# A fused attention and two-layer mixture-of-experts kernel: the order of the gate chain in the first expert layer, its logits, its masks, and how one weight split is cut

## The chip, the cores and the metric

The kernel runs on one core of one Trainium2 chip. The metric is the device time of one execution in microseconds (us). Engines are called as the profile calls them: PE (TensorE, its weight loads apart as PEld), DVE (VectorE), ACT (ScalarE), POOL (GpSimd), SP (the queue that issues most DMAs).

## The reference

Three stages follow each other on 9984 tokens of 256 numbers.

```
scores = (1/S) * z @ z.T                      # S = 2496 tokens, 4 batches
x  = u * (relu(scores)**2 @ v)                # attention
skip = x @ w_skip > 0                         # layer 1: only tokens with skip
logits = x[skip] @ w_gate;  e = argmax;  p = softmax(logits)[e]
x[skip] += p * (relu(x @ w1[e]) @ w2[e])      # F = 1024 hidden, 8 experts
logits2 = x @ w_gate2 + bias[modality]        # layer 2: all tokens
e = argmax;  p = softmax(logits2)[e]
out = p * (relu(x @ w1b[e]) @ w2b[e])
```

The result of layer 1, y, is needed twice: it is added to the token's row, and its product with w_gate2 is added to the logits that the token brought along, which decide the token's expert in layer 2.

## The kernel before, in words

**Stages.** Attention comes first and sorts its tokens by expert into a list in memory, rows1 (tokens that skip layer 1 go to rows2 at once). Layer 1 then takes tiles of 348 rows of one expert (3 groups of 116), layer 2 takes tiles of 512 rows from rows2. All large products are made of three fp32r products of a high and a low half of each operand.

**A tile of layer 1** (`Moe.turn`, `Moe.work`). Two stages of eight parts each: ("h", f) computes block f of the hidden layer (`hidden`, six matmuls at line 766, then `hh` on ACT at 768 and `hl` on DVE at 769), ("o", f) adds block f to y (`out_part`, six matmuls at line 867). PE runs these in the order in which they are written. Between parts stand hooks, named in the dictionary `PLAN`: "next" loads the next tile's rows and w1, "w2" and "w1" split a quarter of the weights into halves (high on ACT, line 665; low of w2 on POOL and low of w1 on DVE, line 666), "x" transposes the next tile's rows (PE at 751, ACT at 755, DVE at 756), "load w2" loads the next w2, and "after" runs one further step of the generator `Moe1.after`.

**`Moe1.after`** finishes the tile before while the present one is computed. In order: copies of y out of PSUM as yS and yh (ACT, 877 and 878, the first instructions of a tile on ACT), the low halves yl (DVE, 881), the transposed logits lt (PE 885, ACT copy 887 to mlt), the rows of y (PE transposes at 894, DVE at 898 writes them into `x_out`; first two groups, then the third), the logits (PE transposes mlt at 904, ACT copy 906, DVE 908 to 910), the first maximum and the exponential (`FirstMax`, lines 109 to 118), the masks and sums of the expert's one-hot rows (920, `counted`, 129 to 136), then the row numbers (PE 148 to 158, DVE 174 to 181, 706). PE products of these steps take turns in two PSUM buffers named m.

**Sending.** `m1.send` stands at the top of the loop body and issues on POOL three scatters of the groups of `x_out` to rows2 (line 680, with small instructions at line 702 in front). The next tile's line 898 writes `x_out` again.

**The loop.** Layer 1 has 16 tiles: two written out in front of a hardware loop, 13 in the loop, one behind it. The last `after` runs inside the first tile of layer 2. Each engine follows its own list of instructions and waits on semaphores; at the end of the loop all engines meet.

**What the change touches.** `constants` (a new constant), `Shared.split` (line 666), `Moe1.PLAN`, `Moe1.after`, the dictionary of the tile in front of the loop, and the call of `m1.after` inside the first tile of layer 2.

Of the kernel before, what the change touches and what calls it, by code (L numbers as in the profile page):

```python
# [53 lines left out]
def constants(nc, pool):  # L54
    k = Consts()
    k.ones = pool.tile([128, 128], BF16, name="ones")
    nc.vector.memset(k.ones, 1.0)
    k.ident = pool.tile([128, 128], F32, name="ident")
    make_identity(nc, k.ident)
    diff = pool.tile([128, 128], F32, name="diff")  # L60
    nc.gpsimd.iota(diff, pattern=[[1, 128]], base=0, channel_multiplier=-1, allow_small_or_imprecise_dtypes=True)
    k.tri = pool.tile([128, 128], BF16, name="tri")
    nc.vector.tensor_scalar(k.tri, diff, 0.0, None, op0=ALU.is_gt)
    k.desc = pool.tile([128, E], F32, name="desc")
    nc.gpsimd.iota(k.desc, pattern=[[-1, E]], base=E, channel_multiplier=0, allow_small_or_imprecise_dtypes=True)
# [555 lines left out]
class Shared:  # L621
# [201 lines left out]
class Moe1(Moe):  # L823
# [5 lines left out]
        ("h", 3): [("w2", 1)],  # L829
        ("h", 4): [("w2", 2), ("after",), ("after",)],  # L830
# [38 lines left out]
    def after(self, lim, current, ps=None):  # L869
# [6 lines left out]
        for d in range(2):  # L876
            nc.scalar.copy(y[:, d], self.y[d])
            nc.scalar.copy(yh[:, d], self.y[d])
        for d in range(2):
            yield  # L880
            nc.vector.tensor_tensor(yl[:, d], y[:, d], yh[:, d].bitcast(F32), op=ALU.subtract)
        yield
        lt_ps = sh.ps_m.tile([2 * E, T], F32, name="m")
        for i, (d, m) in enumerate(((0, yh), (1, yh), (0, yl), (1, yl))):
            nc.tensor.matmul(lt_ps, self.wg[:, d], m[:, d], start=(i == 0), stop=(i == 3))
        lt = self.lt
        nc.scalar.copy(lt[:2 * E], lt_ps)
        yield
        x, xo = self.x_cur, self.x_out[:P]
        for g0 in range(0, G, 2):  # L890
            y_ps = sh.ps_m.tile([128, 2, D], F32, name="m")[:P]
            for g in range(g0, min(g0 + 2, G)):
# [4 lines left out]
            for g in range(g0, min(g0 + 2, G)):  # L897
# [4 lines left out]
        lg_ps = sh.ps_m.tile([128, G, 128], F32, name="m")[:P]  # L902
        for g in range(G):
            nc.tensor.transpose(lg_ps[:, g], lt[:, g * P:(g + 1) * P], k.ident)
        lo = s.tile([128, G, 2 * E], F32, name="mlo")[:P]
        nc.scalar.copy(lo, lg_ps[:, :, 0:2 * E])
        lg = s.tile([128, G, E], F32, name="mlg")[:P]
        nc.vector.tensor_tensor(lg, lo[:, :, 0:E], lo[:, :, E:], op=ALU.add)
        nc.vector.tensor_tensor(lg, lg, x[:, :, C_G1:C_G1 + 1].to_broadcast([P, G, E]), op=ALU.mult)
        nc.vector.tensor_tensor(lg, lg, x[:, :, C_B2:C_B2 + E], op=ALU.add)  # L910
        yield
        fm = FirstMax(nc, s, k, lg, P, G, "b")
        fm.exp()
        oh, sm = fm.hot, fm.total()
        nc.vector.tensor_copy(xo[:, :, C_TID], x[:, :, C_TID])
        nc.vector.reciprocal(xo[:, :, C_G2], sm)
        yield
        if current is not None:
            self.load_rows(current(), self.x_cur)
        nc.vector.tensor_copy(sh.lim, lim.rearrange("p t o -> p (t o)"))  # L920
        mk = self.counted(sh.lim)
        ohb, cum = first_max_done(nc, s, k, oh, mk, P, 1, G, "b")
        yield
        rks = row_counts(nc, s, ps or sh.ps_m, k, ohb, cum, P, 1, G, "b")
        at, mk = row_index(nc, s, rks, ohb, mk, self.carry, P, 1, G, "b")
        self.sc.index(at[:, 0], mk[:, 0])
# [102 lines left out]
def forward_kernel(ctx, tc, zT, v, uT, wg, wg2, mod, bias, w, out, nb=B, mode="reg_based"):  # L1029
# [36 lines left out]
    with ExitStack() as main:  # L1066
# [79 lines left out]
    m2.turn(lambda: (m2, e2, rb), m1.after(m1.table.lim[:, :, ds(n + 2, 1)], None, sh.ps_x), {  # L1146
# [83 lines left out]
```

## Time and profile before

| | |
|---|---|
| median of 3 runs | 1566.53 us (1563.34 to 1571.99) |
| the profiled execution | 1573.25 us |
| its span, first to last instruction | 1571.4 us |
| mean granted TensorE clock over the span | 0.981 |
| PE busy | 1494.9 us, 95% |
| DVE, ACT, POOL busy | 1070.2, 953.5, 598.7 us |
| loop of layer 1 | 795.66 to 1069.98 us of the span, 13 tiles |

All views of the profile come from the profiled execution, which is 6.7 us above the median. Times in the views are counted from the first instruction. A tile of layer 1 is counted here from its first copy of y on ACT (line 877).

### The profile page before, as it was taken

Reading aid. Unit: us, or ns where it says so; the run is one execution under the profiler, and the core shown is the slowest. Engines: PE = TensorE matmul, PEld = TensorE weight load, DVE = VectorE, ACT = ScalarE, POOL = GpSimd, SP = SyncE. Lnnn points to the kernel's source line nnn. Section 1 sums busy time; section 2 is a strip of 40 time slices with the busy share of each in tenths; the row PEclk is TensorE's granted clock in tenths of the full one; section 3 lists DMA queues with packets and bytes.
Section 4 is the critical chain, followed back from the end, with each engine's and each line's share of the span. In section 5 each row is a group of like instructions: output and inputs, shape, how many; then the busy total and the mean of one; then the engine's idle time right before and its main releaser. Section 6 shows DMA issues by size and latency. Waiting matters only on the chain. (4 is left out here: it accounts for less than half of the span.)

```text
span 1571.4 us, 34847 instructions
## 1 busy us (share of the span) xinstructions
PE 1494.9 (95%) x10972; PEld 1286.6 (82%) x10972; DVE 1070.2 (68%) x2562; ACT 953.5 (61%) x1729; POOL 598.7 (38%) x730
## 2 busy tenths in 40 slices
PE   7999999999999999998789898988999999999997
PEld 6878888888887887887788888888888888888886
DVE  7788887888788887776656666666755555545453
ACT  8777777777777777674455455554455455445452
POOL 2022333332222222333634445553553453454353
PEclk9999999999999999999899999999999999999999
DMA  9011211112111200031255444553443343443430
GB/s 356 28 41 56 68 39 44 51 50 91 33 42 61 69 28 27 31 93 49 85 173 158 141 149 151 158 156 107 157 153 128 131 146 124 135 143 121 151 130 23
DMA packets 49696, 160.24 MB, mean 102 GB/s; under 512 B 13285, under 2 KB 15195, under 8 KB 40384
## 3 DMA queue, kind: packets, MB, share of 16 engines
q1 hardware_dynamic: 28720, 124.24, 24.5%
q0 software_dynamic: 20736, 34.71, 6.4%
q8 instruction: 60, 0.98, 0.3%
q14 instruction: 36, 0.29, 0.1%
q10 hardware_dynamic: 144, 0.02, 0.0%
HBM read 124.24 MB, written 46.55 MB: 109 GB/s over the span
## 5 line engine op out<-in xcount | busy, mean ns | idle before, releaser
L680 POOL DMA_INDIRECT rows<-r,ix x160 | 205.3, 1283 | 347.5 <-DVE xs L341 276.1
L328 PE MATMUL o<-ah,vh 64*128 64x512 f32 (+1 forms) x1560 | 312.4, 386 | 9.2 <-DVE xs L341 9.2
L328 PE MATMUL o<-al,vh 64*128 64x512 f32 (+1 forms) x1560 | 304.5, 384 | 0.0
L328 PE MATMUL o<-ah,vl 64*128 64x512 f32 (+1 forms) x1560 | 302.9, 384 | 0.0
L769 DVE SCALAR_TENSOR_TENSOR hl<-ph,hh 128x512 fp32r<-128x512 f32 (+1 forms) x288 | 176.6, 614 | 164.1 <-ACT hh L768 163.1
L285 ACT ACTIVATE t<-s 128x1024 f32<-128x1024 f32 (+2 forms) x201 | 201.2, 1001 | 88.4 <-PE s L282 85.0
L299 DVE TENSOR_TENSOR al<-t,ah 128x1024 fp32r<-128x1024 f32 (+2 forms) x201 | 241.8, 1203 | 17.9
L666 POOL TENSOR_TENSOR w<-w2raw,w 128x512 fp32r<-128x512 f32 x144 | 183.7, 1292 | 179.8 <-issue 163.4
L768 ACT ACTIVATE hh<-ph 128x512 fp32r<-128x512 f32 (+1 forms) x288 | 155.8, 541 | 138.2 <-PE ph L766 118.9
L766 PE MATMUL ph<-mxh,zA 128*128 128x512 f32 (+1 forms) x576 | 217.8, 378 | 3.8 <-PEq L1226 1.8
L766 PE MATMUL ph<-mxh,zB 128*128 128x512 f32 (+1 forms) x576 | 212.4, 369 | 2.8 <-issue 2.8
L766 PE MATMUL ph<-mxl,zA 128*128 128x512 f32 (+1 forms) x576 | 212.6, 369 | 0.0
L297 ACT ACTIVATE t<-t 128x1024 f32<-128x1024 f32 (+2 forms) x201 | 208.1, 1036 | 5.7
L298 DVE CAST ah<-t 128x1024 fp32r<-128x1024 f32 (+2 forms) x201 | 137.1, 682 | 105.6 <-ACT t L297 103.5
L328 PEld LDWEIGHTS o<-ah,vh 64*128 64x128 f32 x1560 | 151.7, 185 | 44.4 <-DVE xs L341 16.8
L328 PEld LDWEIGHTS o<-al,vh 64*128 64x128 f32 x1560 | 151.4, 185 | 26.5
L328 PEld LDWEIGHTS o<-ah,vl 64*128 64x128 f32 x1560 | 148.0, 185 | 27.2
L867 PE MATMUL o<-hh,w 128*128 128x348 f32 x512 | 134.4, 346 | 8.3 <-POOL w L666 8.3
L766 PEld LDWEIGHTS ph<-mxh,zA 128*128 128x128 f32 x576 | 110.9, 193 | 23.6 <-issue 6.4
L282 PE MATMUL s<-zA,zB 64*128 64x512 f32 (+1 forms) x400 | 124.2, 389 | 0.0
L755 ACT CAST mxh<-m 128x512 fp32r<-128x512 f32 (+1 forms) x72 | 37.9, 526 | 140.4 <-PE m L751 140.3
L766 PEld LDWEIGHTS ph<-mxh,zB 128*128 128x128 f32 x576 | 111.0, 193 | 14.6
(229 smaller groups left out, 3056.9 us busy)
## 6 DMA issues: line engine op xcount, KB each, us to landing
w1raw<-in_w SPq DMA_DIRECT2D x36, 1024.0 KB, 9.8
w2raw<-in_w SPq DMA_DIRECT2D x36, 1024.0 KB, 8.3
x_in<-rows SPq DMA_DIRECT2D x20, 520.0 KB
vraw<-in_v SPq DMA_DIRECT2D x20, 512.0 KB, 5.3
ut<-in_uT SPq DMA_DIRECT2D x20, 512.0 KB, 4.1
x_in<-rows SPq DMA_DIRECT2D x16, 364.3 KB
x_cur<-rows SPq DMA_DIRECT2D x16, 364.3 KB
rows<-x_in POOLq DMA_DIRECT2D x8, 536.0 KB, 12.6
```

Of the source, the lines that this page charges most:

```text
L282: nc.tensor.matmul(s[:, i, :n], w[p, k], x[p, q], start=(j == 0), stop=(j == 2))
L285: nc.scalar.activation(t[:, i, :n], s[:, i, :n], AF.Relu, scale=SCALE)
L297: nc.scalar.activation(t[:, i, :n], t[:, i, :n], AF.Square)
L298: nc.vector.tensor_copy(h[:, i, :n], t[:, i, :n])
L299: nc.vector.tensor_tensor(l[:, i, :n], t[:, i, :n], h[:, i, :n].bitcast(F32), op=ALU.subtract)
L328: nc.tensor.matmul(o[half][d][:, :n], w[p, d * 128:d * 128 + 128], x[p, :n], start=(u == 0 and j == at[0]), stop=(u == 9 and j == at[-1]),)
L666: lo_engine.tensor_tensor(l, src, h.bitcast(F32), op=ALU.subtract)
L680: i = tc.nc.gpsimd.indirect_dma_start(out=out, out_offset=bass.IndirectOffsetOnAxis(ap=ix, axis=0), in_=rows, in_offset=None, bounds_check ...
L766: nc.tensor.matmul(ps, w, x, start=(i == 0), stop=(i == len(mms) - 1))
L768: nc.scalar.activation(h, ps, AF.Relu)
L769: nc.vector.scalar_tensor_tensor(l, ps, 0.0, h.bitcast(F32), op0=ALU.max, op1=ALU.subtract)
L867: nc.tensor.matmul(self.y[d], w[:, dd], h[f], start=(f == 0 and i == 0), stop=(f == 7 and i == 2))
```

## The change

It has four parts.

1. `Moe1.after` becomes a list of steps in one of two orders. In 15 of its 16 uses the gate chain comes first: logits, first maximum, one-hot sums and exponential come ahead of the rows of y, and the row numbers between the two halves of the rows. The steps now stand at start, h0, h1, h3, h4, h5, h6, h7, o0, o1 and o2 (before: start, h0, h1, two at h4, h5, h6, h7, o1, o5). Inside the first tile of layer 2 the order of before is kept.
2. The logits are a product of lt with a new 128 by 8 matrix of zeros and ones (`k.pairs`), which adds the high and the low half; an ACT copy and three DVE instructions give way to three on DVE, one for each group.
3. The masks of valid rows and the `drop` values are computed beside the second low half of y.
4. The low half of each quarter of w2 on POOL is two instructions of half the size.

The functions `taken`, `low`, `logits_t`, `rows` and `ranks` hold the code of before for their steps; the last dictionary below belongs to the tile in front of the loop.

```diff
+    k.pairs = pool.tile([128, E], F32, name="pairs")
+    nc.gpsimd.iota(k.pairs, pattern=[[-1, E]], base=0, channel_multiplier=1, allow_small_or_imprecise_dtypes=True)
+    odd = pool.tile([128, E], F32, name="pairs_odd")
+    nc.vector.tensor_scalar(odd, k.pairs, float(E), None, op0=ALU.is_equal)
+    nc.vector.scalar_tensor_tensor(k.pairs, k.pairs, 0.0, odd, op0=ALU.is_equal, op1=ALU.add)
...
-        lo_engine.tensor_tensor(l, src, h.bitcast(F32), op=ALU.subtract)
+        for c in range(2):
+            if i and lo_engine is self.nc.gpsimd:
+                lo_engine.tensor_tensor(l[:, c], src[:, c], h[:, c].bitcast(F32), op=ALU.subtract)
+        if not (i and lo_engine is self.nc.gpsimd):
+            lo_engine.tensor_tensor(l, src, h.bitcast(F32), op=ALU.subtract)
...
-        ("h", 3): [("w2", 1)],
-        ("h", 4): [("w2", 2), ("after",), ("after",)],
+        ("h", 3): [("w2", 1), ("after",)],
+        ("h", 4): [("w2", 2), ("after",)],
         ("h", 5): [("w2", 3), ("load w2",), ("after",)],
         ("h", 6): [("after",)],
         ("h", 7): [("after",)],
-        ("o", 0): [("x", 0)],
+        ("o", 0): [("x", 0), ("after",)],
         ("o", 1): [("w1", 0), ("after",)],
-        ("o", 2): [("w1", 1)],
+        ("o", 2): [("after",), ("w1", 1)],
         ("o", 4): [("x", 1), ("w1", 2)],
-        ("o", 5): [("w1", 3), ("after",)],
+        ("o", 5): [("w1", 3)],
...
+        def logits():
+            lg_ps = sh.ps_m.tile([128, G, E], F32, name="m")[:P]
+            for g in range(G):
+                nc.tensor.matmul(lg_ps[:, g], lt[:, g * P:(g + 1) * P], k.pairs, start=True, stop=True)
+            for g in range(G):
+                nc.vector.scalar_tensor_tensor(
+                    lg[:, g], lg_ps[:, g], x[:, g, C_G1:C_G1 + 1], x[:, g, C_B2:C_B2 + E],
+                    op0=ALU.mult, op1=ALU.add,
+                )
+
+        def masks():
+            gate["drop"] = s.tile([128, G], F32, name="mk_drop")[:P]
+            nc.vector.memset(gate["drop"], 0.0)
+            nc.vector.tensor_copy(sh.lim, lim.rearrange("p t o -> p (t o)"))
+            mk = gate["mk"] = self.counted(sh.lim)[:, 0]
+            nc.vector.tensor_scalar(gate["drop"], mk, -BIG, BIG, op0=ALU.mult, op1=ALU.add)
+            gate["cum"] = s.tile([128, G + 1, E], BF16, name="cumb")[:P]
+            nc.vector.memset(gate["cum"][:, 0], 0.0)
+
+        def first():
+            gate["first"] = FirstMax(nc, s, k, lg, P, G, "b")
+
+        def sums():
+            ohb, cum = s.tile([128, G, E], BF16, name="ohbb")[:P], gate["cum"]
+            gate["ohb"] = ohb
+            nc.vector.tensor_tensor(
+                ohb, gate["first"].hot, gate["mk"].unsqueeze(2).to_broadcast([P, G, E]), op=ALU.mult
+            )
+            for g in range(G):
+                nc.vector.tensor_tensor(cum[:, g + 1], cum[:, g], ohb[:, g], op=ALU.add)
...
+        def close():
+            nc.vector.tensor_copy(xo[:, :, C_TID], x[:, :, C_TID])
+            nc.vector.reciprocal(xo[:, :, C_G2], gate["first"].total())
+            if current is not None:
+                self.load_rows(current(), self.x_cur)
...
+        begin = [taken, lambda: low(0), both(lambda: low(1), masks), logits_t]
+        if gate_first:
+            steps = begin + [logits, first, sums, exp, lambda: rows(0), ranks, both(lambda: rows(2), close)]
+        else:
+            steps = begin + [lambda: rows(0), lambda: rows(2), logits, both(first, exp), both(close, sums), ranks]
...
-        ("h", 6): [("after",), ("after",)],
+        ("h", 6): [("after",)],
         ("h", 7): [("after",)],
         ("o", 0): [("after",)],
-        ("o", 1): [("after",)],
+        ("o", 1): [("after",), ("after",)],
         ("o", 2): [("after",)],
-        ("o", 3): [("x", 0)],
-        ("o", 4): [("w1", 0)],
+        ("o", 3): [("x", 0), ("after",)],
+        ("o", 4): [("after",), ("w1", 0)],
         ("o", 5): [("w1", 1), ("x", 1)],
-        ("o", 6): [("w1", 2), ("after",)],
+        ("o", 6): [("w1", 2)],
...
-    m2.turn(lambda: (m2, e2, rb), m1.after(m1.table.lim[:, :, ds(n + 2, 1)], None, sh.ps_x), {
+    m2.turn(lambda: (m2, e2, rb), m1.after(m1.table.lim[:, :, ds(n + 2, 1)], None, sh.ps_x, False), {
```

## Rows read from the trace of the kernel before

**Rows 1.** Waits of PE, 798 to 1060 us: in all, times, longest.

```profile
PE m L904 <- DVE x_out L898: 25.1, 13, 3.7
```

**Rows 2.** Timeline of ACT: first copy of y, some tiles (start, us).

```profile
795.66 0.45 ACT L877 COPY yS<-o 128x348 f32<-128x348 f32 x1 [2.32 <-DVEq L1136]
...
1025.64 0.45 ACT L877 COPY yS<-o 128x348 f32<-128x348 f32 x1 [1.18 <-PE o L867]
...
1044.62 0.45 ACT L877 COPY yS<-o 128x348 f32<-128x348 f32 x1 [1.69 <-PE o L867]
...
1069.98 0.45 ACT L877 COPY yS<-o 128x348 f32<-128x348 f32 x1 [2.55 <-PEq L1226]
```

**Rows 3.** Busy time in two tiles: PE, PEld, DVE, ACT, POOL, clock, DMA.

```profile
984.75:1003.71 18.96, 18.12 (x120) 17.37 (x120) 13.43 (x43) 10.85 (x25) 10.16 (x13) 1.00 0.50 155
1003.71:1025.64 21.93, 19.50 (x120) 18.88 (x120) 14.14 (x49) 10.85 (x25) 9.93 (x13) 0.92 0.52 155
```

**Rows 4.** Waits of PE inside the first of these tiles, 984.6 to 1004.2.

```profile
PE m L904 <- DVE x_out L898: 0.8, 1, 0.8
```

**Rows 5.** Timeline of a long tile, from 1044.62: scatters, rows of y, PE.

```profile
1050.66 1.28 POOL L680 DMA_INDIRECT rows<-x_out,ix_scatter  x1 [0.19 <-issue]
...
1052.59 0.32 PE L766 MATMUL ph<-mxh,zB 128*128 128x348 f32 x1
...
1055.17 0.87 DVE L898 SCALAR_TENSOR_TENSOR x_out<-m,x_cur 116x256 f32<-116x256 f32 x2 [4.28 <-DMA rows<-x_out,ix_scatter]
...
1056.19 0.87 PE L904 MATMUL m<-ident,mlt 128*116 128x128 f32 x3 [3.28 <-DVE x_out L898]
```

**Rows 6.** Timeline of PE: parts h4 to h6 and the steps between.

```profile
1049.54 0.48 PE L885 MATMUL m<-yh,wg_split 128*16 128x348 f32 x2
...
1050.17 0.60 PE L894 MATMUL m<-ident,yS 128*116 128x128 f32 x4
1050.53 0.41 PE L766 MATMUL ph<-mxh,zA 128*128 128x348 f32 x1
```

**Rows 7.** Timeline of PE around the one full fp32 product (258 columns).

```profile
776.40 0.60 PE L605 MATMUL m<-diag,ones_f 128*128 128x258 f32 x2
776.64 0.51 PE L766 MATMUL ph<-mxh,zA 128*128 128x348 f32 x1
```

**Rows 8.** Timeline of ACT in the short tile that begins at 1025.64.

```profile
1029.94 0.46 ACT L768 ACTIVATE hh<-ph 128x348 fp32r<-128x348 f32 x1
1030.30 0.61 ACT L665 CAST w<-w2raw 128x512 fp32r<-128x512 f32 x1
...
1031.77 0.44 ACT L887 COPY mlt<-m 16x348 f32<-16x348 f32 x1
```

**Rows 9.** Timeline of POOL in the same tile.

```profile
1026.52 0.18 POOL L702 TENSOR_TENSOR ix_scatter<-ix_scatter,ix_zero_scatter 1x3 int32<-1x3 int32 x1 [10.35 <-issue]
...
1032.59 5.02 POOL L666 TENSOR_TENSOR w<-w2raw,w 128x512 fp32r<-128x512 f32 x4
```

**Rows 10.** Timeline of POOL and DVE in the tile in front of the loop.

```profile
780.02 4.99 POOL L666 TENSOR_TENSOR w<-w2raw,w 128x512 fp32r<-128x512 f32 x4
...
783.02 2.03 DVE L908 TENSOR_TENSOR mlg<-mlo 116x24 f32<-116x24 f32 x1 [1.59 <-ACT mlo L906]
785.09 0.18 DVE L909 TENSOR_TENSOR mlg<-mlg,x_cur 116x24 f32<-116x24 f32 x1
```

**Rows 11.** Timeline of DVE in the short tile from 1025.64.

```profile
1036.09 0.51 DVE L769 SCALAR_TENSOR_TENSOR hl<-ph,hh 128x348 fp32r<-128x348 f32 x1
1036.52 1.14 DVE L908 TENSOR_TENSOR mlg<-mlo 116x24 f32<-116x24 f32 x1
```

**Rows 12.** Timeline at the end of the loop: DVE's last instruction.

```profile
1069.01 0.16 DVE L706 TENSOR_TENSOR ix_scatter<-atb,mk 116x3 int32<-116x3 f32 x1
```

**Rows 13.** Waits, 1060 to 1110 us: the tile behind the loop.

```profile
PE m L751 <- DMA x_in<-rows: 3.2, 1, 3.2
```

**Rows 14.** Waits of PE over the whole span.

```profile
PE o L867 <- POOL w L666: 8.3, 2, 7.3
...
PE s L282 <- ACT zA L242: 4.4, 1, 4.4
```

More of the change, by code (lines that the diff above doesn't have):

```diff
@@ L867, in out_part, with after @@
                 nc.tensor.matmul(self.y[d], w[:, dd], h[f], start=(f == 0 and i == 0), stop=(f == 7 and i == 2))
-    def after(self, lim, current, ps=None):
+    def after(self, lim, current, ps=None, gate_first=True):
         nc, k, P, G, T = self.nc, self.k, self.P, self.G, self.T
@@ L875, in after, with taken, low, logits_t @@
         yl = s.tile([128, 2, T], F32R, name="yl")
[L876 to L880, printed above, removed]
-            nc.vector.tensor_tensor(yl[:, d], y[:, d], yh[:, d].bitcast(F32), op=ALU.subtract)
[L882 to L890, printed above, removed]
+        x, xo, lt = self.x_cur, self.x_out[:P], self.lt
+        lg = s.tile([128, G, E], F32, name="mlg")[:P]
+        gate = {}
+        def taken():
+            for d in range(2):
+                nc.scalar.copy(y[:, d], self.y[d])
+                nc.scalar.copy(yh[:, d], self.y[d])
+        def low(d):
+            nc.vector.tensor_tensor(yl[:, d], y[:, d], yh[:, d].bitcast(F32), op=ALU.subtract)
+        def logits_t():
+            lt_ps = sh.ps_m.tile([2 * E, T], F32, name="m")
+            for i, (d, m) in enumerate(((0, yh), (1, yh), (0, yl), (1, yl))):
+                nc.tensor.matmul(lt_ps, self.wg[:, d], m[:, d], start=(i == 0), stop=(i == 3))
+            nc.scalar.copy(lt[:2 * E], lt_ps)
+        def rows(g0):
             y_ps = sh.ps_m.tile([128, 2, D], F32, name="m")[:P]
-            for g in range(g0, min(g0 + 2, G)):
+            gs = range(g0, min(g0 + 2, G))
+            for g in gs:
                 for d in range(2):
@@ L896, in after @@
                     )
-            for g in range(g0, min(g0 + 2, G)):
+            for g in gs:
                 nc.vector.scalar_tensor_tensor(
@@ L900, in after @@
                 )
-            yield
[L902 to L926, printed above, removed]
+        def logits():
[7 more added lines that the diff above has]
+                )
@@ new lines, in sums, with ranks @@
+        def sums():
[6 more added lines that the diff above has]
+                nc.vector.tensor_tensor(cum[:, g + 1], cum[:, g], ohb[:, g], op=ALU.add)
+        def ranks():
+            w, ohb, cum = G * E, gate["ohb"], gate["cum"]
+            flat = lambda t: t.rearrange("p n e -> p (n e)")
+            rk_ps = (ps or sh.ps_m).tile([128, w + E], F32, name="m")
+            nc.tensor.matmul(rk_ps[:P, 0:w], k.tri[:P, :P], flat(ohb), start=True, stop=False)
+            nc.tensor.matmul(rk_ps[:P, 0:w], k.ones[:P, :P], flat(cum[:, 0:G]), start=False, stop=True)
+            nc.tensor.matmul(rk_ps[:, w:], k.ones[:P], cum[:, G], start=True, stop=True)
+            rk = s.tile([128, G, E], F32, name="rkb")[:P]
+            carry = self.carry
+            nc.vector.tensor_tensor(
+                rk, rk_ps[:P, 0:w].rearrange("p (n e) -> p n e", n=G), carry[:P].to_broadcast([P, G, E]), op=ALU.add
+            )
+            nc.vector.tensor_tensor(carry[:, 0], carry[:, 0], rk_ps[:, w:], op=ALU.add)
+            nc.vector.tensor_tensor(rk, rk, ohb, op=ALU.mult)
+            at = s.tile([128, G], F32, name="atb")[:P]
+            nc.vector.tensor_reduce(at, rk, axis=AX.X, op=ALU.add)
+            self.sc.index(at, gate["drop"])
@@ new lines, in close @@
+        def close():
[3 more added lines that the diff above has]
+                self.load_rows(current(), self.x_cur)
+        both = lambda *f: lambda: [i() for i in f]
+        exp = lambda: gate["first"].exp()
+        begin = [taken, lambda: low(0), both(lambda: low(1), masks), logits_t]
[3 more added lines that the diff above has]
+            steps = begin + [lambda: rows(0), lambda: rows(2), logits, both(first, exp), both(close, sums), ranks]
@@ L928, in send @@
+        for step in steps[:-1]:
+            step()
+            yield
+        steps[-1]()
     def send(self):
```

## The prediction

> **What bounds the kernel now.** I began with the waits of PE in the loop of layer 1, as PE is busy 95% of the span. One row holds nearly all of its waiting there: 25.1 us in 13 waits, at the transposes of mlt, for DVE at line 898 [rows 1]. Next come the starts of the tiles [rows 2]. The 13 tiles take 274.32 us (795.66 to 1069.98). They alternate: one that begins at 1025.64 lasts 18.98 us, and six such tiles leave 248.96 - 6 x 18.97 = 135.1 us, or 22.5 each, to the six long ones between 795.66 and 1044.62. The thirteenth is long too and lasts 25.36; the 2.9 above 22.5 are the end of the loop. The table of busy time sets a short tile beside a long one [rows 3]: clock 1.00 against 0.92. In the short one PE waits 0.8 us [rows 4], so its own work and small gaps are 18.96 - 0.8 = 18.2.
>
> The timeline of a long tile shows the cause [rows 5]. PE starts its last matmul before the wait at 1052.59 and its next work at 1056.19, 3.28 us after the end of the former. DVE had stood 4.28 us, until 1055.17, which is 10.5 us into the tile: it may not write `x_out` while scatters of the tile before still read it, and the third of these was issued only at 1050.66. A wait of this length also costs clock: 0.92 of 21.93 means 1.7 us lost to the lower of the two levels (1.2 against 2.4 GHz), where the short tile with 0.8 us of waiting keeps 1.00 [rows 3].
>
> **The order of the steps.** I write times as microseconds into a tile. The rows of y move from h4 and h5 to o0 and o2, so line 898 comes about 13 us into the tile. The scatters move the other way. POOL sat idle for 10.35 us in front of its first touch of the row numbers [rows 9], which are computed at o5; they now come at o1 and `x_out` is complete after o2, near 17. POOL needs 6.1 us from its first touch (1026.52) to its first low half (1032.59), so it is through by 23.4, about 3.7 into the next tile, and their DMA, which took 4.5 us after the last issue in the long tile (1050.66 to 1055.17, [rows 5]), lands near 8, well before 13. Both the 25.1 us and the clock behind them go. SP's loads keep their order; x_cur is asked for at o2 instead of o1 and read at h4 of the next tile.
>
> What is late next? Laid out step by step, the new tile runs as follows.
>
> PE: five parts take 4.92 (1044.62 to 1049.54, [rows 2, 6]), 0.98 each. The four products of lt take 0.63 (1049.54 to 1050.17), four transposes of rows 0.36 [rows 6]. h0 to h3 and lt end near 4.5, h4 near 5.5.
>
> The logits on PE wait for mlt. On ACT, hh of h3 starts at 4.30 into a tile, the w2 cast behind it at 4.66 and takes 0.61 [rows 8]; mlt follows and takes 0.44, so it is ready at 5.7, and the hop from engine to engine comes on top. PE waits **0.3**.
>
> The logits themselves are full fp32 products. The only such product in the trace shows as two instructions, 0.24 from its start to the next matmul [rows 7]; three of them with 8 columns become six small ones. Below, they cost what the three transposes cost (0.27, taken as three of the 0.09 in [rows 6]); above, 3 x 0.24 = 0.72. I take 0.52, being limited like the transposes by the weight load: **+0.25** on PE.
>
> DVE: at h5 it does hl and then the first maximum, whose comparisons read two operands from SBUF. Such an instruction can be held up by POOL: line 908, which lasts 0.18 where POOL is idle (as line 909 does), lasted 2.03 from 783.02 to 785.05, and POOL's four low halves ran from 780.02 to 785.01 [rows 10]. It did not get in between the third and the fourth. The `hl` in front of another such case kept its 0.51, and line 908 there took 1.14 [rows 11]. In the new order the chain runs into POOL's low halves. POOL's half instruction is between 0.63 (half of 5.02 / 4) and 0.80 (with 0.18 of a tiny instruction on top, [rows 9]); I take 0.70, so a quarter costs 1.40. Quarter 0 can start at 4.35, and the four form a train until 9.8 to 10.1. The first maximum is ready at 8.8 and waits about **1.1**. It ends near 10.8, hl of h6 at 11.3, the sums at 12.1.
>
> PE needs the sums for the row numbers at o1, at 11.7: it waits **0.45**. The rows at o2 need the PSUM buffer that line 898 frees; behind hl of h7, the next tile's xl and two of 0.48, that is at about 14.1, and PE is there at 13.7: **0.4**. Nothing on DVE behind this holds up PE: the hl of h5 to h7 are read by o5 to o7, the split of w1 is due only in the next tile. Waits of this size kept the clock at 1.00 [rows 3, 4].
>
> A tile thus takes 18.2 + 0.25 + 0.3 + 0.45 + 0.4 = **19.6**, whether it was short or long.
>
> The Trainium skill, SBUF — State Buffer, section "SBUF: two separate sides", speaks against this order: a DVE instruction with two SBUF inputs and a GpSimd instruction that reads SBUF exclude each other, and whichever starts first holds the port for its whole instruction. The rows agree that they exclude each other, and differ on how long: 2.03 is more than one instruction of 1.25 [rows 10]. By the page's rule the chain would get in after one half, 0.6 earlier, and lose again to the second half, which leaves the tile between 19.4 and 19.6; by the row it is 19.6.
>
> **The other parts.** The masks are the same instructions and a memset, moved to h1, where POOL has no low halves to do. The three DVE instructions for the logits replace three. ACT loses a copy of 0.2 that PE did not wait for. In layer 2 the halves add about 0.15 to each quarter on POOL, whose low halves PE never waited for there: the two waits in the whole span are at line 867, in the tiles around the start of layer 1 [rows 14]. There they could change by 0.6 either way. The new constant is three small instructions while PE waits 4.4 for its first operands [rows 14]; without that cover it would be 0.6.
>
> **Around the loop.** The end of the loop waits for DVE, whose last instruction is the row number at 1069.01 [rows 12]; with that step gone from o5 the 2.9 become about 2.4. Behind the loop PE waits 3.2 for the next rows [rows 13], which come after the scatters sent at the loop's end; 0.5 to 1.0 us of row transposes move behind that wait. I set these two against each other.
>
> **The sum.** 13 x 19.6 + 2.4 = 257.2, against 274.3: 17 less. From the profiled execution, 1573.25, that gives 1556; it is 6.7 above the median, so for the median I predict 1566.5 - 17 = **1549.5**.
>
> **The rivals.**
>
> *The chain hides.* If DVE gets in early enough for PE to wait only for mlt, a tile takes 18.65 to 19.2: the loop ends at 245 to 252 and the kernel at 1537 to 1544. For it: POOL's quarters wait for ACT's casts, which may open gaps. Against it: the 2.03 of [rows 10].
>
> *The gain goes into new waits.* POOL's half costs 0.80, the train lasts until 10.8, and the waits at o1 and o2 grow to 1.5 or more together: 20.1 to 20.9 a tile, 1556 to 1566, up to no change. For it: the loss of 0.83 and more in each short tile that line 908 already shows [rows 11].
>
> *Slower: POOL's train comes late.* If the scatters still run at the head of a tile, as now until 6.95 [rows 9], because POOL doesn't send before the next tile begins, the low halves end at 12.5, the first maximum at 13.4, the sums at 14.7. PE waits 3.0 at o1 and 0.4 at o2, a tile takes 22.3, and the loop 292: 1584, more if the clock falls as in the long tiles. It decides from 20.9 a tile, that is from scatters that end after about 5.7. Against it: POOL stood idle for the row numbers alone [rows 9], and these come 5 us earlier.
>
> Losing POOL's port again and again, with each of the seven two-operand instructions of the chain, would do the same without lateness; but only two halves are still to come when the chain starts, 1.4 in all.
>
> *It doesn't do what it says:* DVE waits for the scatters at o0 as well. Then PE's waits stay near 25 us, 1566. The DMA landed 10.5 into the tile with a late send, and 13 is later, so little speaks for it.
>
> **How the numbers follow.** Forecast 0.45 (19.2 to 20.1 a tile, 1544 to 1556), the hidden chain 0.25, new waits 0.17, slower 0.10, not done 0.03. A measurement tells 0.5% (7.8 us) from no change, so faster means below 1558.7: 0.45 + 0.25 + 0.06 = 0.76; within 0.14; slower 0.10. The range runs from 18.65 a tile, with only the wait for mlt, to 20.5, with the costlier halves: 1537 to 1561.
>
> **What would show it.** Right: in the waits of PE the 25.1 at line 904 is gone, DVE no longer waits for `x_out`'s DMA, every tile is alike near 19.6, the clock is 1.00 in the loop, small waits appear at the logits (line 885's copy), at the row numbers and at the row transposes of o2, and two-operand instructions of the first maximum last about 1 us. Wrong: tiles that still alternate, scatters that start after the tile's beginning, or PE waits of more than 2 us at the row numbers.

## The result

The changed kernel takes 1547.6 us (median of four runs, 1546.72 to 1548.68), the kernel before 1566.76 beside it (1563.34 to 1571.99): a ratio of 0.9875, with an interval of 0.9847 to 0.9904. That is 19 us less, where 17 were predicted. Its profiled execution took 1547.99, with a span of 1546.2. Side by side once more, in five rounds, the two gave 1551.04 and 1576.02, a ratio of 0.9847 (0.9823 to 0.987).

In the changed file the lines have moved: hidden product 775, hl 778, second product 876, low half of y 895, copy of the transposed logits 901, row transposes 908, `x_out` 912, logits 919 and 921, first maximum 114 to 120, sums 941 and 945, products of the row numbers 951 to 953, their last instruction 715, scatters 689, POOL's touches 711, low halves of w2 on POOL 673. Busy time by stretch in the profile after (duration, PE, PEld, DVE, ACT, POOL, clock, DMA share, GB/s): the first tile, the 13 of the loop, the tile behind it, the rest.

```profile
770.77:796.80 26.03, 20.90 (x126) 19.68 (x124) 18.50 (x64) 10.88 (x25) 13.21 (x17) 0.93 0.41 124
796.80:1048.25 251.45, 240.97 (x1574) 229.43 (x1574) 186.83 (x598) 138.01 (x312) 140.53 (x222) 1.00 0.54 165
1048.25:1071.17 22.92, 20.87 (x122) 19.70 (x123) 14.28 (x47) 10.88 (x24) 13.66 (x23) 0.85 0.43 139
1071.17:1546.20 475.03, 468.42 (x2416) 394.74 (x2414) 247.88 (x570) 234.23 (x440) 224.43 (x392) 1.00 0.38 129
```

The loop took 274.32 [rows 2] and takes 251.45, 22.9 less, at a clock of 1.00. Inside it the tiles no longer alternate: the first takes 20.51 us, eleven take 18.90 to 18.99, and the thirteenth 22.46, with the loop's end. Waits in the loop (in all, times, longest):

```profile
POOL ix_scatter L711 <- DMA rows<-x_out,ix_scatter: 18.4, 12, 2.9
...
ACT zA L670 <- DMA w1raw<-in_w: 6.0, 9, 1.5
PE m L908 <- DVE x_out L912: 6.0, 13, 0.6
...
PEld m L919 <- issue: 3.8, 13, 0.3
...
PE ph L775 <- PEq L1281: 3.3, 1, 3.3
```

The 25.1 us of [rows 1] are gone, and DVE waits for no scatter; POOL does, where nobody waits for it. One tile, from 987.89: DVE's chain and its rows of `x_out`, POOL with the scatters on either side of the tile's start, and PE at the logits and the row numbers.

```profile
996.46 0.17 DVE L114 TENSOR_REDUCE mxb<-mlg 116x3 f32<-116x24 f32 x1
996.66 0.75 DVE L115 TENSOR_TENSOR dfb<-mlg,mxb 116x24 f32<-116x24 f32 x1
997.45 0.66 DVE L116 SCALAR_TENSOR_TENSOR hotb<-dfb,desc 116x24 f32<-116x24 f32 x1
...
999.16 0.55 DVE L945 TENSOR_TENSOR cumb<-cumb,ohbb 116x8 bf16<-116x8 bf16 x3
...
1000.59 0.87 DVE L912 SCALAR_TENSOR_TENSOR x_out<-m,x_cur 116x256 f32<-116x256 f32 x2
...
1002.86 0.48 DVE L912 SCALAR_TENSOR_TENSOR x_out<-m,x_cur 116x256 f32<-116x256 f32 x1
```

```profile
989.53 1.28 POOL L689 DMA_INDIRECT rows<-x_out,ix_scatter  x1 [0.19 <-issue]
992.43 5.64 POOL L673 TENSOR_TENSOR w<-w2raw,w 128x256 fp32r<-128x256 f32 x8 [1.63 <-issue]
1000.16 0.18 POOL L711 TENSOR_TENSOR ix_scatter<-ix_zero_scatter 1x3 int32<-1x3 int32 x1 [2.09 <-DMA rows<-x_out,ix_scatter]
...
1005.04 1.26 POOL L689 DMA_INDIRECT rows<-x_out,ix_scatter  x1 [1.23 <-DVE zB L675]
```

```profile
993.64 0.75 PE L919 MATMUL m<-pairs,mlt 128*116 128x8 f32 x6
994.24 0.41 PE L775 MATMUL ph<-mxh,zA 128*128 128x348 f32 x1
...
999.85 0.18 PE L951 MATMUL m<-ohbb,tri 116*116 116x24 bf16 x1
```

Two instructions of the first maximum last 0.75 and 0.66 us where 0.18 is usual; the sums end at 999.71, 11.82 into the tile, and PE comes to the row numbers at 11.96 and does not wait. The last scatter of the tile before goes out at 1.64, and POOL sees it landed at 12.27 (1000.16). DVE overwrites the first two groups of `x_out` from 1000.59 on, and the third, the one that this scatter reads, at 1002.86.

To place what changed outside the loop too, this table takes from each profile the start of the first tile, its length, that of the loop, of the tile behind, and the rest of the span. The lower rows are the experiments.

| kernel | start | first tile | loop | tile behind | rest | span |
|---|---|---|---|---|---|---|
| before | 770.36 | 25.30 | 274.32 | 22.03 | 479.4 | 1571.4 |
| after | 770.77 | 26.03 | 251.45 | 22.92 | 475.0 | 1546.2 |
| e9, after again | 768.69 | 29.17 | 252.87 | 23.41 | 475.0 | 1549.1 |
| e1 | 770.44 | 25.79 | 294.65 | 20.44 | 476.9 | 1588.2 |
| e2 | 772.96 | 26.75 | 251.69 | 21.77 | 474.7 | 1547.9 |
| e3 | 771.91 | 26.89 | 253.83 | 21.85 | 474.8 | 1549.3 |
| e4 | 771.70 | 23.79 | 261.18 | 21.03 | 475.0 | 1552.7 |
| e5 | 771.62 | 28.96 | 249.40 | 20.82 | 480.6 | 1551.4 |
| e6 | 771.59 | 29.68 | 245.95 | 20.98 | 479.4 | 1547.6 |
| e7 | 769.53 | 30.43 | 259.17 | 20.67 | 479.7 | 1559.5 |
| e8 | 770.05 | 29.97 | 277.67 | 20.47 | 481.5 | 1579.7 |
| e10, e6 again | 767.63 | 30.45 | 245.83 | 21.18 | 479.3 | 1544.4 |
| e11 | 771.15 | 34.79 | 253.63 | 23.81 | 479.7 | 1563.1 |
| e12 | 772.64 | 29.26 | 295.61 | 21.50 | 476.8 | 1595.8 |

Between the two profiles the loop gives 22.9 us, the rest 4.4, and the start, the first tile and the tile behind take 2.0 back: 25.2 in all. The medians are only 19.2 apart because the profiled execution of before lies 6.5 above its median and that of after 0.4 above its own.

### The profile page after: what moved, and what is told of

It reads as the page before. It is cut to its first block, busy times and chain, and to the rows that moved or that the text cites. A ratio compares the mean times of both kernels' runs of the same rounds, so it can differ in the third digit from the quotient of the medians.

```text
span 1546.2 us, 35423 instructions
## 1 busy us (share of the span) xinstructions
PE 1489.3 (96%) x11020; PEld 1282.1 (83%) x11020; DVE 1077.8 (70%) x2580; ACT 949.7 (61%) x1713; POOL 619.9 (40%) x875
## 3 DMA queue, kind: packets, MB, share of 16 engines
q1 hardware_dynamic: 28720, 124.24, 25.1%
## 5 line engine op out<-in xcount | busy, mean ns | idle before, releaser
L673 POOL TENSOR_TENSOR w<-w2raw,w 128x256 fp32r<-128x256 f32 x288 | 203.9, 744 | 193.8 <-issue 178.4
L775 PE MATMUL ph<-mxh,zA 128*128 128x512 f32 (+1 forms) x576 | 213.0, 370 | 5.6 <-PEq L1281 3.9
```

The costliest lines, as they stand in the source:

```text
L673: lo_engine.tensor_tensor(l[:, c], src[:, c], h[:, c].bitcast(F32), op=ALU.subtract)
L775: nc.tensor.matmul(ps, w, x, start=(i == 0), stop=(i == len(mms) - 1))
```

## The experiments

**e1: the change without its order.** The order of the steps and the list of what runs in which part are those of before; logits by the 0/1 product, masks in part 1 and halved low splits stay.

```diff
-    def after(self, lim, current, ps=None, gate_first=True):
+    def after(self, lim, current, ps=None, gate_first=False):
```

> The changed kernel with the order of the steps and the hooks of before in all tiles of layer 1; the product with the 0/1 matrix, the early masks and the halved splits of w2 stay. My theory: the order is what counts, so the tiles alternate again, PE waits at the logits (now line 919) for the rows of y on DVE, which wait for the scatters of x_out. Masks and logits leave DVE about 1 us earlier at the end of a tile, so the row numbers and the scatters may start up to 1 us earlier: PE's wait 15 to 25 us in the loop, the loop 262 to 274 us, the kernel 1556 to 1567. Rival (the smaller parts bring the gain): short and long tiles are alike, kernel below 1552.

1591.06 us against 1573.21, a ratio of 1.0135 (1.01 to 1.0169). The waits of PE and of DVE in the loop:

```profile
PE m L919 <- DVE x_out L912: 36.8, 13, 4.5
...
DVE x_out L912 <- DMA rows<-x_out,ix_scatter: 49.3, 16, 5.5
```

The wait of [rows 1] is back and larger, and so the loop takes 294.65. Without the order no gain is left: the other three edits cost 18 us in the old order. Which of them does was asked again in e8 and e12.

**e2: whole low halves of w2 in the new order.**

```diff
-        for c in range(2):
-            if i and lo_engine is self.nc.gpsimd:
-                lo_engine.tensor_tensor(l[:, c], src[:, c], h[:, c].bitcast(F32), op=ALU.subtract)
-        if not (i and lo_engine is self.nc.gpsimd):
-            lo_engine.tensor_tensor(l, src, h.bitcast(F32), op=ALU.subtract)
+        lo_engine.tensor_tensor(l, src, h.bitcast(F32), op=ALU.subtract)
```

> The changed kernel with each low quarter of w2 on POOL as one instruction again. My theory: the comparisons of the first maximum wait for a whole instruction of 1.25 us instead of a half of 0.70; the sums come up to 0.7 us later, PE waits up to 0.5 at the row numbers and 0.4 to 0.9 at the rows of o2. A tile 18.95 to 19.7, the kernel 1547 to 1557. Rival (DVE doesn't get in between POOL's instructions, so that only the end of the train counts): the train is even 0.6 us shorter, a tile not above 18.95, the kernel 1545 to 1548.

1549.95 (1547.7 to 1551.69), a ratio of 0.9869 (0.9834 to 0.9904) to before, like the changed kernel's. The tiles take 18.96 to 19.05 instead of 18.90 to 18.99. DVE's first two-operand instruction of the chain now waits through one whole instruction of POOL, the last of the tile, and the next one does not wait:

```profile
923.65 1.29 POOL L671 TENSOR_TENSOR w<-w2raw,w 128x512 fp32r<-128x512 f32 x1 [0.40 <-issue]
```

```profile
923.68 1.29 DVE L115 TENSOR_TENSOR dfb<-mlg,mxb 116x24 f32<-116x24 f32 x1
925.01 0.18 DVE L116 SCALAR_TENSOR_TENSOR hotb<-dfb,desc 116x24 f32<-116x24 f32 x1
```

Held up 1.11 us once, or 0.57 and 0.48: it comes to the same. In both kernels the hold ends with POOL's last low half, 10.0 into the tile here (from 914.91) and 10.2 in the change (992.43 + 5.64), and the sums end at 11.90 and 11.82. The halving is worth at most 0.1 us a tile.

**e3: the old way to the logits in the new order** (three transposes, a copy on ScalarE, a sum of the two halves).

```diff
-                nc.tensor.matmul(lg_ps[:, g], lt[:, g * P:(g + 1) * P], k.pairs, start=True, stop=True)
+                nc.tensor.transpose(lg_ps[:, g], lt[:, g * P:(g + 1) * P], k.ident)
...
+            nc.scalar.copy(lo, lg_ps[:, :, 0:2 * E])
+            nc.vector.tensor_tensor(lg, lo[:, :, 0:E], lo[:, :, E:], op=ALU.add)
```

> The changed kernel with the logits made as before: three transposes, an ACT copy and three DVE instructions. My theory: PE's own work is the same within 0.2 us a tile, but the ACT copy stands behind a cast of w2 and two or three of the DVE instructions read two operands from SBUF while POOL's low halves run, so the chain ends 1 to 2 us later and PE waits 0.5 to 1.5 us at the row numbers and the rows of o2: tile 19.5 to 20.5, kernel 1554 to 1567. Rival (the way of the logits is worth only PE's time): tile 18.9 to 19.0, kernel 1547 to 1549.

1549.92 (1548.07 to 1551.09), a ratio of 0.9865 (0.9832 to 0.9899); tiles of 18.85 to 18.99 behind the first. Here I was wrong: the 0/1 product by itself is worth nothing that shows, neither in the tile nor in the chain, whose sums end 11.81 into a tile (from 991.95), as with the product.

**e4: row numbers late again**, at o5 as before, all else as in the change.

```diff
-        ("o", 1): [("w1", 0), ("after",)],
+        ("o", 1): [("w1", 0)],
-        ("o", 5): [("w1", 3)],
+        ("o", 5): [("w1", 3), ("after",)],
```

> The changed kernel with the row numbers back at o5, behind the rows and the load of x_cur: the scatters start at the head of the next tile as before, while the rows of y are still written at o0 and o2. My theory: the late writing of the rows alone avoids the DMA wait (DVE waits less than 1 us a tile for x_out), but POOL's low halves start near 7 us into a tile and end near 12.5, the first maximum loses more to them, and the rows at o0 come later: tile 19.5 to 21, kernel 1555 to 1575. Rival (late writing is all that matters): tile 18.5 to 19.0, kernel 1542 to 1548. Second rival (early scatters are what matters): DVE waits for x_out's DMA as before and the tiles alternate, 1560 or more.

1557.02 (1555.18 to 1557.69), a ratio of 0.9916 (0.9883 to 0.9949). DVE still waits for no scatter; most tiles take 19.7. The theory held, and the rows of one tile (from 912.44) say why it is slower: POOL sends the scatters late again, so its low halves start 8.16 into the tile instead of 4.54, and the first instruction of the first maximum lasts 3.97 us, where it lasted 0.75 in the change (3.96 to 4.60 in eleven of the 13 tiles).

```profile
920.60 5.59 POOL L673 TENSOR_TENSOR w<-w2raw,w 128x256 fp32r<-128x256 f32 x8
927.01 0.18 POOL L711 TENSOR_TENSOR ix_scatter<-ix_zero_scatter 1x3 int32<-1x3 int32 x1 [0.82 <-DMA rows<-x_out,ix_scatter]
```

```profile
921.56 3.97 DVE L115 TENSOR_TENSOR dfb<-mlg,mxb 116x24 f32<-116x24 f32 x1
...
928.29 0.51 DVE L765 TENSOR_TENSOR mxl<-m,mxh 128x348 fp32r<-128x348 f32 x1
928.71 0.86 DVE L912 SCALAR_TENSOR_TENSOR x_out<-m,x_cur 116x256 f32<-116x256 f32 x2
```

The sums end at 15.41 instead of 11.82, the next tile's split x (line 765) stands behind them on DVE, and PE has a new wait for it:

```profile
PE m L760 <- DVE mxl L765: 8.3, 11, 1.0
```

So a late write of `x_out` removes the wait for the scatters without early numbers. Here it comes at 16.27, with all scatters landed by 14.57; that a write at 12.7, as in the change, would be late enough with scatters sent this late is not shown. Early numbers are worth 0.8 a tile, some 10 us of the loop with its end (261.18 against 251.45, of which 3.4 in the last tile), and for another reason than the landing: POOL is done with its scatters sooner, and its low halves end before they hold DVE's chain for long.

**e5: all rows first, numbers behind them** (all rows of `x_out` at o1, numbers at o2).

```diff
-            steps = begin + [logits, first, sums, exp, lambda: rows(0), ranks, both(lambda: rows(2), close)]
+            steps = begin + [logits, first, sums, exp, lambda: rows(0), lambda: rows(2), both(close, ranks)]
```

> The changed kernel with the second half of the rows of y at o1 and the row numbers (with the load of x_cur) at o2. The second half then takes the PSUM buffer of the logits, free long before, and doesn't wait for DVE's first half. My theory: the waits of 0.44 a tile at these transposes go, nothing else changes: tile 18.5, kernel 1541 to 1544. Rival (DVE is the bound and the wait only moves to the row numbers): tile 18.9 to 19.0, kernel 1547 to 1549. Second rival: the scatters start 0.5 to 1 us later, their DMA ends after 12.7 us into the next tile, and DVE waits for it at line 912: tile 19.3 or more, 1552 or more.

1552.35 (1549.12 to 1553.42), a ratio of 0.9872 (0.9848 to 0.9895): no gain. DVE waits for no scatter in the loop here either, so a landing too late is not the reason. The tiles came down to 18.80, 2 us in the loop, and the rest of the span grew from 475.0 to 480.6; e10 shows by what.

**e6: the logits a part later as well**: e5, with logits at h5, first maximum at h6, sums and exponentials at h7.

```diff
-        ("h", 4): [("w2", 2), ("after",)],
+        ("h", 4): [("w2", 2)],
...
+            steps = begin + [logits, first, both(sums, exp), lambda: rows(0), lambda: rows(2), both(close, ranks)]
```

> As the run with rows before numbers, and the logits one part later (h5, the first maximum at h6, the sums at h7), so that PE doesn't wait for the copy of lt. My theory: 0.3 more a tile is gained: 18.2, kernel 1537 to 1541. Rival (the chain comes too late on DVE): PE waits at the transposes of the next rows or at the row numbers, tile 18.9 or more, kernel 1547 or more.

1550.61 (1545.65 to 1552.09), a ratio of 0.9861 (0.9832 to 0.989). The tiles take 18.53, and still no gain beyond the change shows.

**e7: the kernel before with half of the loop's w1 load.** It leaves out half of w1's bytes, so the products use mixed weights; the work of the engines is the same.

```diff
+        n = 1024 if i == 0 and self.less else 2048
-        self.nc.sync.dma_start(self.raw[i], w.rearrange("o p w -> p (o w)")[:, i * 2048:(i + 1) * 2048])
+        self.nc.sync.dma_start(self.raw[i][:, 0:n], w.rearrange("o p w -> p (o w)")[:, i * 2048:i * 2048 + n])
```

> The kernel before, with the loop's load of w1 cut to its first half (the second half of w1 stays that of an earlier expert, so the loop loads 0.5 MB less a tile and computes with mixed weights). My theory of the wait: the scatters of x_out share the DMA engines with the load of w1 that is issued just ahead of them, and land when it is done; with half the load they land some 2 us earlier, DVE waits for x_out less than 1 us a tile, PE's wait at line 904 falls from 25 us to 5 to 12, the tiles are alike at about 18.9 and the kernel takes 1540 to 1552. Rival (the scatters are slow by themselves): tiles alternate between 19 and 22 as before, 1563 or more.

1558.36 (1554.95 to 1561.34), a ratio of 0.9914 (0.9887 to 0.994), between the two expectations. The waits of PE and DVE in its loop:

```profile
PE m L906 <- DVE x_out L900: 17.6, 13, 2.7
...
DVE x_out L900 <- DMA rows<-x_out,ix_scatter: 19.2, 13, 3.7
```

The wait at line 904 of [rows 1] falls from 25.1 to 17.6, and the loop from 274.3 to 259.2, with no step moved. Long tiles of 21.5 to 22.2 come every third or fourth time only, between tiles of 18.4 to 19.4. So the scatters of before landed late in good part because the load of w1 ran beside them, but not for that alone.

**e8: halved low splits in the kernel before**, the edit of e2 turned round.

```diff
-        lo_engine.tensor_tensor(l, src, h.bitcast(F32), op=ALU.subtract)
+        for c in range(2):
+            if i and lo_engine is self.nc.gpsimd:
+                lo_engine.tensor_tensor(l[:, c], src[:, c], h[:, c].bitcast(F32), op=ALU.subtract)
```

> The kernel before with only the halved splits of w2 on POOL. It asks why the changed kernel with the order of before was 18 us slower than before. My theory: not the halves, as POOL's train is off the path in this order: PE's wait at line 904 20 to 30 us, kernel within 0.5% of before. Rival (the halves let DVE and POOL interleave so that something of the order of before comes later): PE's wait 35 us or more, kernel 1% slower.

1581.98 (1578.44 to 1584.97), a ratio of 1.0058 (1.0024 to 1.0091): 10 us slower. Only 3.4 of them are in the loop (277.67); the first tile takes 4.7 more and the rest of the span 2.1. I read it as a price of the halves in the old order, and e12 tested that.

**e9 to e12** ran together, five rounds each, beside a kernel before at 1576.02. **e9: the changed kernel again**, with no edit.

> The changed kernel itself, as the measure for the three kernels beside it, since the stages behind this layer took 475 to 477 us in the profiles of one group of runs and 479 to 482 in those of the other. Theory: a ratio of 0.985 to 0.990 to the kernel before, and tiles of 18.9 to 19.0 in the loop.

1551.04 (1550.85 to 1552.75). The loop takes 252.87, and the rest of the span 475.0 to the tenth as in the first profile of this kernel. That the rest differs between groups of runs, as I had written, is wrong: the kernel decides it.

**e10: e6 again**, with the diff shown there.

> The kernel of the run e6 once more: logits at h5, the first maximum at h6, sums and exponentials at h7, all rows of x_out at o1, the row numbers at o2. Its tiles took 18.53 us in that profile, the changed kernel's 18.9. Theory: the 0.4 of each of 13 tiles is real and what hid it was the difference between groups of runs, so it is 4 to 6 us faster than the changed kernel beside it. Rival: what the tiles lose comes back behind the loop, and the two are within 2.5 us of each other.

1549.99 (1544.64 to 1552.1) against 1551.04: the rival holds. The loop is 7.0 us shorter, and the rest of the span is 4.3 longer, in this profile as in that of e6. (The profiled execution, 1546.25, lies 3.7 under the median; where its other runs are longer has no trace.) The row of the loop, DVE at its end, and PE at the start of the next layer:

```profile
798.08:1043.91 245.83, 237.71 (x1574) 229.07 (x1574) 181.28 (x598) 138.99 (x312) 145.51 (x222) 1.00 0.56 168
```

```profile
1067.79 0.16 DVE L715 TENSOR_TENSOR ix_scatter<-atb,mk_drop 116x3 int32<-116x3 f32 x1 [5.61 <-issue]
...
1068.47 0.68 DVE L765 TENSOR_TENSOR mxl<-m,mxh 128x512 fp32r<-128x512 f32 x1
...
1069.21 0.80 PE L775 MATMUL ph<-mxl,zA 128*128 128x512 f32 x1 [2.81 <-DVE mxl L765]
```

At the change of layers DVE stands 5.61 us in front of its last row number, with nothing that the profile shows to wait for; the split of the next layer's x queues behind it, and PE waits 2.81. The clock is 0.96 in the 40 us that begin there, which is the rest of the 4.3. In e5 and e6 the same instruction stood 5.72 and 5.35 us. In the change it runs 0.1 us behind the one before it: there the last row numbers come a part earlier, before that place.

**e11: the order with the masks in their new place, and nothing else of the change**, by the edits of e2 and e3 together.

```diff
-        for c in range(2):
...
+        lo_engine.tensor_tensor(l, src, h.bitcast(F32), op=ALU.subtract)
...
-                nc.tensor.matmul(lg_ps[:, g], lt[:, g * P:(g + 1) * P], k.pairs, start=True, stop=True)
+                nc.tensor.transpose(lg_ps[:, g], lt[:, g * P:(g + 1) * P], k.ident)
```

> The changed kernel with both the whole low-half subtractions of w2 and the logits by transposes, ScalarE copy and sum: of the change only the order of the chain and the place of the masks are left. Theory: the order carries the gain, so the time is within 4 us of the changed kernel beside it, with tiles of 18.9 to 19.1. Rival: the two parts cover for each other, each harmless alone because the other is there; then it is 8 us or more slower, with tiles of 19.5 or more.

The median is 1564.04 (1558.57 to 1567.42), 13 us over the changed kernel beside it, though either edit alone was free (e2, e3). By the time the rival is right, by the loop it is not: 253.63 against 252.87, with tiles of 18.7 to 19.45 between its first and its last. Between the profiles of e11 and e9 14.0 us are missing, and the table says where: 2.5 ahead of the layer, 5.6 in its first tile, 0.8 in the loop, 0.4 behind it, 4.8 in the rest. The first tile shows waits for hl and the rows of x (1.8 and 1.0 in e9); in the rest there is one pause, some 30 us before the end, in layer 2:

```profile
PE ph L771 <- DVE hl L774: 5.3, 1, 5.3
...
PE m L756 <- DMA x_in<-rows: 3.7, 1, 3.7
```

```profile
1529.54 0.17 DVE L1041 COPY meta<-meta 128x8 f32<-128x8 f32 x1 [2.91 <-PEq L1277]
1533.58 0.67 PE L771 MATMUL ph<-mxh,zA 128*128 128x512 f32 x1 [3.11 <-issue]
```

The kernel before has that pause too:

```profile
1542.50 0.40 PE L766 MATMUL ph<-mxh,zB 128*128 128x512 f32 x1 [2.20 <-issue]
```

e7 and e8 also have it (2.6 and 3.7), and their rest is 479.7 and 481.5; the change, e1 to e4, e9 and e12 have it not, and theirs is 474.7 to 476.9. So the rest of the span depends on two pauses at places where the program goes over to other code, and neither is work of the steps that were moved; the first stands in front of a moved step where that step comes late. The first tile is less certain than the rest: in the two profiles of the changed kernel itself it differs by 3.1 us (26.03 and 29.17).

**e12: e1 with whole low halves**, the edits of e1 and e2 together.

```diff
-    def after(self, lim, current, ps=None, gate_first=True):
+    def after(self, lim, current, ps=None, gate_first=False):
...
-        for c in range(2):
...
+        lo_engine.tensor_tensor(l, src, h.bitcast(F32), op=ALU.subtract)
```

> The kernel of the run e1 (all of the change but the order) with whole low-half subtractions of w2 again: of the change only the 0/1 product for the logits and the place of the masks are left, in the old order. Theory: the halves carried about 10 of the 18 us that e1 lost, as they cost 10 in the kernel before; the time is then 6 to 12 us above the kernel before. Rival 1: the halves are all of it, and the time is within 4 us of the kernel before. Rival 2: the halves only collide with the old product; the time stays 15 us or more above it.

1601.5 (1594.48 to 1605.53), a ratio of 1.0162 (1.0134 to 1.0189): still 25 us over before. The loop takes 295.61, like e1's 294.65. My theory on the halves falls: they are not the price of e1. It lies with what e12 keeps: the product for the logits, the place of the masks, and two small DVE instructions (the copy of the token's number and the reciprocal of the sum) that come one step later with the change's code. In its loop the waits are 33.3 us on PE and 42.7 for the scatters on DVE, and the clock is 0.92, against 25.1 and 0.94 in before's loop:

```profile
PE m L915 <- DVE x_out L908: 33.3, 13, 5.0
...
DVE x_out L908 <- DMA rows<-x_out,ix_scatter: 42.7, 14, 6.0
```

Which of them, and how it makes DVE wait longer for the scatters, no run here tells.

## Why the prediction was right, step by step

**What bound the loop** was read rightly: with `x_out` written 12.7 into the tile (predicted: about 13) the wait for the scatters is gone, and the clock in the loop is 1.00. e1 shows that without the order nothing of the gain remains, e11 that the order with the place of the masks has the loop at 253.6, and e4 that a late write (there at 16.3) does away with the wait though the scatters go out late.

**The tile: 18.95 in the mean against 19.6.** The terms, as measured:

| term | predicted | measured | from |
|---|---|---|---|
| PE's own work | 18.2 | 18.1 | 18.95 less the three waits below |
| product for the logits | +0.25 | 0 | e3: 18.85 to 18.99 without it |
| wait for mlt | 0.3 | 0.3 | 3.8 in 13, the weight load at line 919 |
| wait at the row numbers | 0.45 | 0.06 | two waits in the loop, 0.8 together, both in its first tile |
| wait at the rows of o2 | 0.4 | 0.46 | 6.0 in 13, line 908 |

Two terms were too large. The product takes 0.60 from its start to the next matmul (993.64 to 994.24), near the 0.52 taken, and the transposes of e3 take 0.27 there (997.70 to 997.97); but e3's tile is no shorter, as PE's wait at line 908 grows from 0.46 to 0.60 in it. Where the rest of the 0.33 goes is not shown. At the row numbers each side was off by 0.3: the sums came at 11.8 instead of 12.1, PE at 12.0 instead of 11.7. Together these are 0.64 a tile, 8 us of the loop. By size the outcome lies on the edge of the rival in which the chain hides (18.65 to 19.2 a tile, 245 to 252 for the loop); the mechanism is the forecast's, since the chain is held up as foreseen and ends just in time.

**POOL's hold on the chain: 1.05 us against 1.1.** DVE lost 0.57 and 0.48 to POOL's last two halves of about 0.70. The Trainium skill, SBUF — State Buffer, section "SBUF: two separate sides", says that whichever of the two starts first gets the shared port for its whole instruction. The changed kernel's tiles agree: DVE got in behind the seventh half and lost again to the eighth, as the page's rule had it in the prediction. e4 and the first tile of e2 show more than that: the same instruction took 3.97 us while halves of 0.70 ran back to back, which is the time of five of them, and 3.85 us beside whole ones of 1.25, of which three passed it. Alternate turns are thus not assured, as [rows 10] had already shown. The hold was short because the chain came when two halves were left, as the prediction had it; e4 is what its rival with POOL's train coming late looks like, at 19.7 a tile where the rival had 22.3. A slip in another rival: 0.83 is how long line 908 lasts in one short tile (at 828.85), so the loss there is 0.65.

**When the scatters land: near 8 predicted, 12.3 measured.** This step was mis-sized. POOL is through with the last one at 2.92 instead of 3.7, but the 4.5 us to landing that I carried over from a long tile do not hold in the new order. Median times from issue to landing, 820 to 1040 us, in the kernel before and in the changed one:

```profile
rows<-x_out,ix_scatter POOLq DMA_INDIRECT x33, 4.5
```

```profile
w1raw<-in_w SPq DMA_DIRECT2D x11, 1024.0 KB, 11.5
...
rows<-x_out,ix_scatter POOLq DMA_INDIRECT x34, 9.8
```

The load of w1 started with the tile before the change too; here it is in the long tile from 1044.62 of before and in the changed kernel's tile from 987.89:

```profile
1045.08 0.36 SPq L657 DMA_DIRECT2D w1raw<-in_w  x1
```

```profile
987.91 0.37 SPq L662 DMA_DIRECT2D w1raw<-in_w  x1
```

What moved is the scatters: the last goes out 1.6 us behind the load instead of 5.6 (1050.66), and lands no earlier for it, about 10 us after the load was issued before (with the 4.5) and 12.25 after. In the changed loop it lands with the load: in seven of the nine tiles in which ACT waits for w1, POOL sees the scatter landed within 0.25 us of ACT's start, as here (POOL at 1000.16):

```profile
999.92 1.14 ACT L670 CAST zA<-w1raw 128x512 fp32r<-128x512 f32 x2 [0.73 <-DMA w1raw<-in_w]
```

e7 shows by half a load that such a load delays the scatters; how it does is not shown.

The prediction also took the wait of [rows 5] for the landing of the third scatter. Each group of `x_out` waits for its own scatter only: in the short tile from 984.75 of before, DVE writes the first group 1.71 us after the third scatter is issued, and the second after a wait. In [rows 5] the wait was thus for the first scatter, sent at 1047.23.

```profile
990.41 1.26 POOL L680 DMA_INDIRECT rows<-x_out,ix_scatter  x1 [0.18 <-PE m L885]
```

```profile
992.12 0.48 DVE L898 SCALAR_TENSOR_TENSOR x_out<-m,x_cur 116x256 f32<-116x256 f32 x1 [1.09 <-PE m L894]
993.25 0.48 DVE L898 SCALAR_TENSOR_TENSOR x_out<-m,x_cur 116x256 f32<-116x256 f32 x1 [0.65 <-DMA rows<-x_out,ix_scatter]
```

So the margin that I counted as 5 us is 2.7 for the third group (1000.16 to 1002.86). The late landing cost nothing here.

**Around the loop.** The loop's end gives 3.5 instead of 2.4: 22.46 less 18.95, with 3.3 that the profile puts down to PE's own sequencer, where [rows 12] had led me to DVE. The two edits behind the loop that I set against each other came to +0.9 in that tile: the 3.2 of [rows 13] are gone, a pause of 1.8 (for issue) is new, and the clock is 0.85, where it was 1.00 in that tile of before.

**The sum.** Loop 17 predicted, 22.9 measured, for the two mis-sized terms (8 us), less the loop's end (1.1) and the first tile of the loop (20.51, 1.6 over the others, with waits of 1.0 at the loop's entry and 0.8 at the row numbers). That the total came nearer, 1549.5 against 1547.6, is luck. The rest of the span, for which the prediction put nothing, gave 4.4: the pause in layer 2, and the clock behind it, 0.88 in the last 31 us of before against 0.96. The start, the first tile and the tile behind the loop took 2.0 back. And the loop of before was read in an execution 6.5 above its median, that of after in one 0.4 above, which takes 6.1: 22.9 + 4.4 - 2.0 - 6.1 = 19.2. How much of the 6.5 is in before's loop cannot be told, as its other runs have no trace.

## What to carry to other kernels

Where an engine waits to overwrite a buffer that a transfer still reads, writing later can be enough; sending earlier (here the row numbers) must be priced by its own effect on the engines' order. Here it did not bring the landing forward; it paid because POOL, done with the scatters, ran most of its low halves before DVE's chain came to them. A landing time taken from one order does not hold for another that sends at another moment beside a large load: price it as a range, and count the margin left for each part of the buffer. And compare stages, not only totals: here edits that shortened the loop by 7 us gained nothing, and two edits each free alone cost 13 us together, in both cases by pauses and waits outside the loop.

## What was not expected of the hardware

The last indirect scatter of a tile took 4.5 us to land when it went out some 5.6 us behind a load of 1 MB, and 9.8 when it went out 1.6 us behind it; the load itself took 11.5. A DVE instruction of 0.18 with two SBUF operands lasted 3.97 beside POOL's back-to-back halves of 0.70. The rest of the span behind this layer came back to the tenth for one kernel (475.0 and 475.0; 479.4 and 479.3 for e6) and moved by 4 to 7 us between kernels whose steps there are nearly the same, by pauses of 2 to 6 us on PE or DVE that the profile puts down to issue or to a sequencer, where the code goes over to another part. What causes them is not shown. Over all runs here the kernel before varied by 18 us (1563.34 to 1581.09), the changed one by 6 (1546.72 to 1552.75). Part of this may lie with the chip, as e1 to e4, e5 to e8 and e9 to e12 ran on three different ones; in the last group alone before varied by 9.6 and the changed kernel by 1.9, and this has no cause that was shown.
